# Seven half products for eight in part of a first FFN product, with sums and copies moved to GpSimd

## The chip, the cores and the metric

The kernel runs on one core of a Trainium2 chip. The metric is the device time of one execution in microseconds (us), as the median of several runs. The engines are TensorE (PE; PEld is its weight load), VectorE (DVE), ScalarE (ACT), GpSimd (POOL) and SyncE (SP). Each runs its own instructions in order and waits on semaphores for the others.

## The reference

Attention for 8 batches of 8 heads, with 512 local and 32 global tokens of head dimension 64. Local tokens see the global ones and a window of 32 on both sides; global tokens see everything. The result, 4352 tokens of 512 values, goes through a feed-forward network:

```
s_ll = where(|i - j| <= 32, scale * q_l @ k_l.T, -1e9);  s_lg = scale * q_l @ k_g.T
out_l = softmax([s_lg, s_ll]) @ [v_g, v_l]
out_g = softmax(scale * q_g @ [k_g, k_l].T) @ [v_g, v_l]
x = [out_g, out_l] as (tokens, 512)
h = x @ w_in                 # 512 -> 2048
g = h / (1 + exp(-1.702 h))
out = g @ w_out              # 2048 -> 512
```

The matrix products take bf16 operands and sum in f32. Inputs and outputs are f32.

## The kernel before

A batch has 512 local tokens; the global tokens of all batches are one more "batch" of 256, number B = 8, done last. Attention works on head groups of four heads; batch b has two, `a` and `c` (class `Wide`, lines 500 to 604). For each: `Tk` and `Tq` transpose loaded keys and queries on DVE, `kcopy`, `qcopy` and `ext` copy parts of them into place, `S` forms scores on PE in two rounds, `X` takes the exponential on ACT, `M` multiplies by the window mask (DVE, or POOL where `eng` says so), `U` and `Gm` multiply by the values on PE, `R` forms reciprocals of the sums (DVE), `XL` and `G` write the normalised result into `xL[b]`, the activations of the FFN, and `xG`.

The FFN has two stages per batch.

- The *h stage* (lines 1087 to 1109): sixteen blocks, `h_step(i, fc)`, of four matmuls of 128 x 128 weights by 512 tokens (`h_mm`, L615), then gelu on ACT into `gTs[i][:, fc]` (`gelu`, L620). Between blocks stand transposes and copies for the second head group of batch i+1 and the first of batch i+2, and sums of gelu outputs, `g_sums`.
- The *output stage*, `phase_o(i)` (lines 1017 to 1085): the second product, as two `Pair`s. A `Pair` forms a 2 x 2 block product with seven half products instead of eight (Strassen's scheme in Winograd-like form); it needs sums of blocks of w_out (`wsum`, formed once) and of gelu outputs. `g_sums(i, lo, hi, which)` forms four kinds of the latter for groups lo to hi-1, where group g holds blocks 2g and 2g+1: kinds 0, 1 and 3 are 256 columns per group, kind 2 is 512 (L696, L699, into `gs0` to `gs3`). Products 3 and 4 need no sum, product 1 kind 0, product 6 kind 1, products 5 and 2 kind 2, and product 7 kind 3. Products 3 and 4 are added up by `m3` (a copy on ACT) and `z` (DVE) before products 5 and 2 may go on into the same PSUM bank (`px`); `zm` reads product 1 before 6 and 7 may add to `py`; `sub`, `evict` and `add` finish. Between the products stand the attention steps of batch i+1 and the first scores of batch i+2.

The order of work is written out by hand: with `manual_schedule` each engine's queue holds its instructions in the order in which the program calls them. So an instruction that waits holds all behind it on its engine. PSUM is given out in turn: four banks of `psP` (tag `p`: `hp`, `ov`, `og`, `px`, `py`) and two double banks (`spair`, scores). `gT` and the four `gs` tiles exist once, `ob` (the output rows) three times.

POOL's queue in the middle of the kernel holds the mask multiply of the first head group's first round (`a2.M(0, nc.gpsimd)`, L1053) and the DMA issues of `loads_after` (L961): nine for the values of batch i+3, and for batch i+4 the two of keys and queries, which wait until the h stage's transposes have freed their buffer.

The steps that the change touches, as they stand in an h stage of batches 2 to 7 and in `phase_o`:

```
if fc == 1: c.Tk(); c.Tq(); c.ext((3,))
if fc in (3, 5, 7): c.ext(((3, 5, 7).index(fc),), on_act)
if fc == 9: a2.T(); transpose_g(2 * i + 4, 2 * i + 6); a2.ext()
if fc in (4, 8, 12): g_sums(i, fc // 2 - 2, fc // 2)
if fc == 13: g_sums(i, 6, 7)
...
a.UG(); c.S(0); a.R(); g_sums(i, 7, 8, (0,)); a.XL(0); g_sums(i, 7, 8, (1, 2))
a.XL(1); g_sums(i, 7, 8, (3,)); p0.mm(3, 4, 1); c.X(0); p0.m3(); p0.z(); a.G()
c.M(0); c.S(1); c.X(1); p0.mm(6); p0.zm(); c.M(1); p0.mm(5, 2); p0.sub(); p0.evict(); p0.mm(7)
```

Of the kernel before, what the change touches and what calls it, by code (L numbers as in the profile page):

```python
# [12 lines left out]
F32 = mybir.dt.float32  # L13
# [7 lines left out]
def kernel(  # L21
# [12 lines left out]
    nc = tc.nc  # L34
# [77 lines left out]
    def on_act(out_, in_):  # L112
        nc.scalar.activation(out_, in_, AF.Copy)  # L113
# [170 lines left out]
    def spair():  # L284
        return [psS.tile([128, 2, 512], F32, name="s4", tag="s%d" % i) for i in range(2)]
# [4 lines left out]
    class Quad:  # L290
        def __init__(self, Q):
            self.Q = Q
            self.b, self.u = divmod(Q, 2)
            if self.u == 0:
                xL[self.b] = att.tile([128, NKC, Sl], BF16, name="xL", bufs=2)
            self.x = xL[self.b]
            self.v = v_view(self.b, 5 if self.b else 4)[:, self.u]
            self.qt = qtiles[Q % 4]
            self.q = self.qt.bitcast(BF16).rearrange("p t (r e) -> p t r e", e=2)
            self.qg = qgT[:, Q, :32].bitcast(BF16).rearrange("p (s e) -> p s e", e=2)  # L300
            self.kg = kgT[:, Q].bitcast(BF16).rearrange("p (s e) -> p s e", e=2)
            self.E = [None, None]
            self.bk = {}
            self.st = {}
            self.pt = None
            self.gr = 1
# [312 lines left out]
    def gelu(out_, in_):  # L619
        nc.scalar.activation(out_, in_, AF.Gelu_apprx_sigmoid)  # L620
# [12 lines left out]
    def exp_table():  # L633
        nc.scalar.activation(spot[:, 0:1], spot[:, 1:2], AF.Exp)
# [5 lines left out]
    def h_step(i, fc):  # L640
# [4 lines left out]
        h_mm(i, fc, hp, range(NKC))  # L645
        h_act(i, fc, hp)

    def o_mm(i, st, out=True, part=range(4)):
        tci, f4 = divmod(st, 4)
        first = (i, tci) not in ops  # L650
        if first:
            ops[i, tci] = pbank("op")
        op = ops[i, tci]
        for fc in [4 * f4 + n for n in part]:
            nc.tensor.matmul(op, lhsT=gTs[i][:, fc, tci * 128 : tci * 128 + 128],  # L655
                             rhs=w_out_sb[:, fc, :], start=(first and fc == 4 * f4), stop=(fc == FC - 1))
        if f4 == 3 and 3 in part and out:
            o_out(i, tci, op)
# [18 lines left out]
        t = gTs[i].rearrange("p (g e) t -> p g e t", e=2)  # L677
        return [t[:, :, e, h * n // 2 : h * n // 2 + n // 2] for h in range(2) for e in range(2)]

    def g_sums(i, lo, hi, which=(0, 1, 2, 3)):  # L680
        n = width(i)
        if i not in sums:
            if i < B:
                sums[i] = [moe.tile([128, FC // 2, w * HT], BF16, name="gs%d" % k)
                           for k, w in enumerate((1, 1, 2, 1))]
            else:
                room = [ld.tile([128, 2, 16 * D], BF16, name=x).rearrange("p a b -> p (a b)")
                        for x in ("rk", "rq", "rk")]
                sums[i] = [x.rearrange("p (g t) -> p g t", g=FC // 2)
                           for x in (room[0][:, :1024], room[0][:, 1024:], room[1], room[2][:, :1024])]  # L690
        a11, a12, a21, a22 = parts_of(i)
        t = gTs[i].rearrange("p (g e) t -> p g e t", e=2)
        g = slice(lo, hi)
        for k in which:
            if k == 2:
                nc.vector.tensor_tensor(sums[i][2][:, g, :n], t[:, g, 0, :n], t[:, g, 1, :n], ALU.add)  # L696
            else:
                x, y, op = {0: (a11, a22, ALU.add), 1: (a21, a11, ALU.subtract), 3: (a12, a22, ALU.subtract)}[k]
                nc.vector.tensor_tensor(sums[i][k][:, g, : n // 2], x[:, g], y[:, g], op)  # L699

    class Pair:
        def __init__(self, i, tt, banks=None):
# [4 lines left out]
        def mm(self, *ks):  # L707
            i, tt = self.i, self.tt
            n = width(i) // 2
            a11, a12, a21, a22 = parts_of(i)  # L710
            s = sums[i]
            for k in ks:
                lv, rv, where = {
                    1: (s[0], wsum[0], 2), 2: (s[2][:, :, n : 2 * n], b11, 1), 3: (a11, wsum[1], 0),
                    4: (a22, wsum[2], 1), 5: (s[2], b22, 0), 6: (s[1], wsum[3], 3), 7: (s[3], wsum[4], 2),
                }[k]
                if self.apart:
                    out_ = self.banks[where][:, :HM]
                else:
                    if k == 3:  # L720
                        self.x = self.banks[0] if self.banks else pbank("px")
                    if k == 1:
                        self.y = self.banks[1] if self.banks else pbank("py")
                    out_ = (self.y if where > 1 else self.x)[:, where % 2 * HM : where % 2 * HM + HM]
                for g in range(FC // 2):
                    nc.tensor.matmul(out_, lhsT=lv[:, g, tt * 128 : tt * 128 + 128], rhs=rv[:, g, :],  # L726
                                     start=(g == 0 and k in ((1, 3, 4, 6) if self.apart else (1, 3))), stop=(g == FC // 2 - 1 and k in (2, 5, 6, 7)),
                                     skip_group_check=True)

        def m3(self, eng="act"):  # L730
            self.zz = moe.tile([128, 2, HM], F32, name="zz")
            if eng == "act":
                on_act(self.zz[:, 0], self.x[:, :HM])
            else:
                nc.vector.tensor_copy(self.zz[:, 0], self.x[:, :HM])

        def z(self):
            nc.vector.tensor_add(self.zz[:, 0], self.zz[:, 0], self.x[:, HM:])

        def zm(self):  # L740
            nc.vector.tensor_add(self.zz[:, 1], self.zz[:, 0], self.y[:, :HM])
# [5 lines left out]
        def sub(self):  # L747
            nc.vector.tensor_sub(self.zz, self.zz, self.x.rearrange("p (h m) -> p h m", h=2))  # L748

        def add(self):  # L750
            nc.vector.tensor_add(self.ob[:, 0:4:3], self.zz, self.y.rearrange("p (h m) -> p h m", h=2))
# [265 lines left out]
    def phase_o(i):  # L1017
        b = i + 1
        a, c = nq[b]
        a2, c2 = quads_of(b + 1)  # L1020
        p0, p1 = Pair(i, 0), Pair(i, 1)
        exp_table()
        a.UG()
        c.S(0)
        a.R()
        g_sums(i, 7, 8, (0,))
        a.XL(0)
        g_sums(i, 7, 8, (1, 2))
        a.XL(1)
        g_sums(i, 7, 8, (3,))  # L1030
        p0.mm(3, 4, 1)
        c.X(0)
        p0.m3()
        p0.z()
        a.G()
        c.M(0)
        c.S(1)
        c.X(1)
        p0.mm(6)
        p0.zm()  # L1040
        c.M(1)
        p0.mm(5, 2)
        p0.sub()
        p0.evict()
        p0.mm(7)
        p0.add()
        p0.store()
        if a2:
            c.UG()
            c.R()  # L1050
            a2.S(0)
            a2.X(0)
            a2.M(0, nc.gpsimd)  # L1053
            loads_after(i + 1)
        else:
            pt = spair()
            c.U(0, bank(pt, 0))
            c.U(1, bank(pt, 2))
            c.U(2, bank(pt, 3))
            c.Gm(bank(pt, 1))  # L1060
            c.R()
        c.XL(0)
        if a2:
            c.XL(1)
            c.G()
        p1.mm(3, 4)
        p1.m3()
        p1.z()
        if not a2:
            c.XL(1)  # L1070
            c.G()
        p1.mm(1, 6)
        p1.zm()
        if a2:
            a2.S(1)
            a2.X(1)
        p1.mm(5, 2)
        p1.sub()
        p1.evict()
        gelu_table()  # L1080
        p1.mm(7)
        p1.add()
        if a2:
            a2.M(1)
        p1.store()

    for i in range(1, B):
        if i > 1:
            for fc in range(FC):
                h_step(i, fc)  # L1090
                if i == 2 and fc == 0:
                    weight_sums(1, 2)
                if i + 1 < B:
                    c = nq[i + 1][1]
                    if fc == 1:
                        c.Tk()
                        c.Tq()
                        c.ext((3,))
                    if fc in (3, 5, 7):
                        c.ext(((3, 5, 7).index(fc),), on_act)  # L1100
                    if fc == 9 and i + 2 < B:
                        a2 = quads_of(i + 2)[0]
                        a2.T()
                        transpose_g(2 * i + 4, 2 * i + 6)
                        a2.ext()
                if fc in (4, 8, 12):
                    g_sums(i, fc // 2 - 2, fc // 2)
                if fc == 13:
                    g_sums(i, 6, 7)
        if i == 1:  # L1110
            phase_o1()
        elif i + 1 < B:
            phase_o(i)
# [88 lines left out]
```

## Time and profile before

| what | us |
|---|---|
| median of 3 runs | 287.18 (286.78 to 289.01) |
| the profiled execution | 288.3 |
| its span, first to last instruction | 286.5 |
| PE busy | 278.6 |
| DVE busy | 204.7 |
| ACT busy | 183.9 |
| POOL busy | 95.1 |
| one h stage of batches 3 to 7, PE | 13.8 |
| one output stage of batches 2 to 5, PE | 17.7 |
| granted TensorE clock, mean | 0.998 of full speed |

The span is the profiled execution's own; what lies around it is 1.8 us. Lines such as L615 are lines of the kernel as printed above; a helper's line stands for all its calls. In a line of a timeline the first number is the start in us from the span's start, the second the time until the last of the merged instructions ends; in brackets stands how long the engine had been idle and what released it. In the chain of waits each line is a piece of the path that ended last: start, length, engine, what is written, source line and the number of instructions.

### The profile page before, as it was taken

The page shows a single profiled execution, that of the slowest core. Times are in us where ns is not written, and L with a number is a line of the kernel's source. Part 1 is how long each engine was busy: PE and PEld are TensorE (multiplying, and loading weights), DVE is VectorE, ACT ScalarE, POOL GpSimd, SP SyncE. Part 2 cuts the span into 40 slices and gives each one's busy share as a digit, 9 for nine tenths or more (in the row PEclk, how much of TensorE's full clock was granted, in tenths as well). Part 3 has the DMA queues.
Part 4 walks back from the last instruction along what each step waited for, and adds up shares of the span by engine and source line. Part 5 has one row for each costly group of instructions (what it writes and reads, how often), then busy time and mean ns, then how long its engine had stood idle before and what let it go on. Part 6 is the DMA issues. An engine that isn't in the chain of part 4 may idle for free.

```text
span 286.5 us, 8846 instructions
## 1 busy us (share of the span) xinstructions
PE 278.6 (97%) x3727; PEld 179.0 (62%) x3727; DVE 204.7 (71%) x494; ACT 183.9 (64%) x297; POOL 95.1 (33%) x142
## 2 busy tenths in 40 slices
PE   7899999989999999999999999999999999999995
PEld 6554445434554478646884488647874589448884
DVE  6680468678689899579957998679957697363352
ACT  3857657558678775688458783878468761864331
POOL 8974550765936100940068002910040000000001
PEclk9999999999999999999999999999999999999999
DMA  7999995899999901794029903880122002200213
GB/s 203 174 194 210 203 141 83 148 212 134 152 168 194 152 3 39 82 188 83 2 77 153 159 6 76 79 87 5 28 51 73 2 3 76 73 0 2 73 35 115
DMA packets 59351, 28.23 MB, mean 99 GB/s; under 512 B 47472, under 2 KB 49776, under 8 KB 59312
## 3 DMA queue, kind: packets, MB, share of 16 engines
q0 software_dynamic: 51760, 17.83, 55.1%
q1 hardware_dynamic: 7120, 9.18, 11.6%
q10 hardware_dynamic: 432, 0.66, 0.7%
q8 instruction: 29, 0.48, 0.7%
q14 instruction: 10, 0.08, 0.1%
HBM read 36.31 MB, written 8.91 MB: 158 GB/s over the span
## 4 chain that ended last, share of the span: by engine, by line
PE 77%; DMA 10%; POOL 7%; issue 3%; DVE 1%; ACT 1%; POOLq 0%
PE hp L615 33%; PE px L726 13%; PE py L726 9%; PE x L726 6%; PE op L655 5%; PE s L560 5%; PE ov L586 5%; DMA rq<-in_q_l_dram 4%; DMA w_out_sb<-in_moe_w_out_dram 3%; DMA rk<-in_k_l_dram 2%; POOL w_in_sb L260 2%; POOL v L250 1%; POOL mask L225 1%; POOL v L98 1%; PE og L597 1%
## 5 line engine op out<-in xcount | busy, mean ns | idle before, releaser
L615 PE MATMUL hp<-xL,w_in_sb 128*128 128x512 bf16 x480 | 105.6, 379 | 1.5 <-ACT gT L620 1.3
L615 PEld LDWEIGHTS <-w_in_sb 128*128 128x128 bf16 x576 | 56.0, 98 | 61.6 <-issue 2.0
L620 ACT ACTIVATE gT<-hp 128x512 bf16<-128x512 f32 x120 | 69.7, 597 | 23.6 <-PE hp L615 22.0
L571 ACT ACTIVATE e<-s 128x1016 bf16<-128x1016 f32 (+1 forms) x56 | 53.2, 1003 | 25.3 <-PE s L560 25.3
L726 PEld LDWEIGHTS <-gs 128*128 128x128 bf16 x480 | 46.3, 98 | 6.4
L699 DVE TENSOR_TENSOR gs<-gT 128x512 bf16<-128x512 bf16 (+1 forms) x90 | 30.3, 363 | 17.5 <-ACT gT L620 17.3
L576 POOL TENSOR_TENSOR e<-e,mask 128x1760 bf16<-128x1760 bf16 x4 | 13.3, 3319 | 83.4 <-ACT e L571 83.4
L98 POOL DMA_DIRECT2D v<-in_v_l_dram x40 | 31.1, 780 | 14.9 <-PE og L597 4.3
L726 PE MATMUL py<-wsum,gs 128*128 128x256 bf16 x240 | 30.3, 273 | 0.0
L655 PE MATMUL op<-w_out_sb,gT 128*128 128x512 bf16 x128 | 29.5, 380 | 0.0
L576 DVE TENSOR_TENSOR e<-e,mask 128x1712 bf16<-128x1712 bf16 (+1 forms) x24 | 25.2, 1048 | 4.2 <-ACT e L571 4.1
L512 DVE STREAM_TRANSPOSE kT<-rk 128x512 f32<-128x512 f32 x14 | 14.6, 1045 | 17.4 <-DMA rk<-in_k_l_dram 17.4
L759 POOL DMA_DIRECT2D out_dram<-ob x2 | 1.2, 597 | 68.2 <-ACT ob L113 68.0
L655 PEld LDWEIGHTS <-gT 128*128 128x128 bf16 x128 | 11.8, 98 | 14.0
L726 PEld LDWEIGHTS <-gT 128*128 128x128 bf16 x192 | 18.0, 98 | 2.9
L726 PE MATMUL px<-w_out_sb,gT 128*128 128x256 bf16 x160 | 19.2, 273 | 0.0
L726 PE MATMUL px<-w_out_sb,gs 128*128 128x256 bf16 x160 | 19.1, 273 | 0.0
L471 DVE TENSOR_TENSOR xL<-ov,rs 128x512 bf16<-128x512 f32 x27 | 17.9, 686 | 0.7 <-PE ov L438 0.3
L696 DVE TENSOR_TENSOR gs<-gT 128x1024 bf16<-128x1024 bf16 (+1 forms) x30 | 17.3, 578 | 0.0
L560 PEld LDWEIGHTS <-kT 32*128 32x128 bf16 x672 | 12.5, 93 | 6.8 <-issue 5.7
L113 ACT ACTIVATE ob<-px 128x512 f32<-128x512 f32 x10 | 6.0, 598 | 15.2 <-DVE zz L748 15.2
L560 PE MATMUL s<-q,kT 32*128 32x160 bf16 (+1 forms) x448 | 14.7, 246 | 0.0
(154 smaller groups left out, 359.7 us busy)
## 6 DMA issues: line engine op xcount, KB each, us to landing
out_dram<-ob SPq DMA_DIRECT2D x128, 64.0 KB, 2.4
rq<-in_q_l_dram POOLq DMA_DIRECT2D x5, 512.0 KB, 8.0
rk<-in_k_l_dram POOLq DMA_DIRECT2D x5, 512.0 KB, 10.4
v<-in_v_l_dram POOLq DMA_DIRECT2D x24, 96.0 KB, 4.8
w_in_sb<-in_moe_w_in_dram POOLq DMA_DIRECT2D x8, 256.0 KB, 8.1
w_out_sb<-in_moe_w_out_dram POOLq DMA_DIRECT2D x4, 512.0 KB, 10.4
rk<-in_k_l_dram POOLq DMA_DIRECT2D x5, 256.0 KB, 7.9
rq<-in_q_l_dram POOLq DMA_DIRECT2D x5, 256.0 KB, 8.0
```

The lines of the kernel that those rows point to most:

```text
L98: nc.gpsimd.dma_start(out=vt[0:n, hs, c, :D], in_=vs[FIRST[c] : FIRST[c] + n, hs])
L471: nc.vector.tensor_mul(self.x[:, 2 * self.u + h, :], self.st[1 + h], self.st["rs"])
L512: nc.vector.transpose(flat[:, 0:Sl].rearrange("p (r t) -> p t r", t=16), loaded[self.b][0][:, self.u].bitcast(F32))
L560: nc.tensor.matmul(bank(self.ps, j)[:, at : at + n], lhsT=self.k[p, KEYS[c] : KEYS[c] + 128, e], rhs=qs[p, :, :, e], start=(e == 0), stop= ...
L571: nc.scalar.activation(self.E[rnd][:, 2 * i : 2 * i + 2, :n], self.ps[i][:, :, :n], AF.Exp, scale=scale)
L576: eng.tensor_mul(e, e, mask[:, rnd : rnd + 1, :n].to_broadcast([128, 4, n]))
L615: nc.tensor.matmul(hp[:, : width(i)], lhsT=w_in_c[:, fc // 4, kc, fc % 4 // 2, :, fc % 2], rhs=(xL[i] if i < B else xG)[:, kc, :], start=( ...
L620: nc.scalar.activation(out_, in_, AF.Gelu_apprx_sigmoid)
L655: nc.tensor.matmul(op, lhsT=gTs[i][:, fc, tci * 128 : tci * 128 + 128], rhs=w_out_sb[:, fc, :], start=(first and fc == 4 * f4), stop=(fc = ...
L696: nc.vector.tensor_tensor(sums[i][2][:, g, :n], t[:, g, 0, :n], t[:, g, 1, :n], ALU.add)
L699: nc.vector.tensor_tensor(sums[i][k][:, g, : n // 2], x[:, g], y[:, g], op)
L726: nc.tensor.matmul(out_, lhsT=lv[:, g, tt * 128 : tt * 128 + 128], rhs=rv[:, g, :], start=(g == 0 and k in ((1, 3, 4, 6) if self.apart els ...
```

## The change

For batches 3 to 7, blocks 4 to 7 of the h stage (groups 2 and 3) are formed with seven half products per pair of blocks (class `HPair`) and not as four `h_step`s: 28 matmuls of 256 columns for 16 of 512. This takes sums of blocks of w_in (`h_weight_sums`, once, on POOL, in the output stage of batch 2's program; they lie in `early`, a buffer that is only used at the start and in the last batch), sums of blocks of `xL` (`x_sums`, four instructions on DVE, called in `phase_o` after `p1.zm()`), and four further DVE instructions and a copy on ACT per batch (`z`, `zm`, `sub`, `add`, `m3`). Gelu of these four blocks is two instructions of 1024 columns, `inner` from PSUM and `outer` from the `ob` buffer that held the sums.

The h stage of batches 3 to 7 is written anew (`h_some`). Kinds 2 and 3 of the sums of groups 0 and 1, kinds 1, 2 and 3 of groups 2 to 5 and kind 2 of group 6 go to POOL; groups 2 to 5 are summed in one instruction per kind after `outer`. The copies `kcopy`, `qcopy` and part 3 of `ext` for the second head group of batch i+1, and all copies for the first of batch i+2, go from DVE to POOL, the latter after the sums. The h stage of batch 2, the sums of group 7 and the last batch are as they were.

```diff
+    HG = (2, 3)
+    w_h = w_in_sb.rearrange("p o k (g m e) -> p o k g m e", m=128, e=2)[:, 1]
+    w11, w12, w21, w22 = (w_h[:, 2 * k : 2 * k + 2, :, :, e] for e in range(2) for k in range(2))
...
+    def h_weight_sums(eng=nc.gpsimd):
+        for t, x, y, op in zip(wh, (w11, w21, w11, w21, w12), (w22, w22, w12, w11, w22),
+                               (ALU.add, ALU.add, ALU.add, ALU.subtract, ALU.subtract)):
+            eng.tensor_tensor(t, x, y, op)
...
+    def x_sums(i):
...
+        for o, x, y, op in zip(xs["d"], (x11, x12, x21), (x22, x22, x11), (ALU.add, ALU.subtract, ALU.subtract)):
+            nc.vector.tensor_tensor(o, x, y, op)
+        nc.vector.tensor_tensor(xs["s"], t[:, :, :HT], t[:, :, HT:], ALU.add)
+        xs["r"] = (x11, x22)
+
+    class HPair:
+        def __init__(self, i):
+            self.i = i
+            self.x, self.y = spair()
+            self.zz = moe.tile([128, 4, HM], F32, name="ob", bufs=3).rearrange("p (u h) t -> p u h t", u=2)
+
+        def mm(self, *ks):
+            for k in ks:
+                lv, rv, where = {
+                    1: (wh[0], xs["d"][0], 2), 2: (wh[1], xs["r"][0], 1), 3: (w11, xs["d"][1], 0),
+                    4: (w22, xs["d"][2], 1), 5: (wh[2], xs["r"][1], 0),
+                    6: (wh[3], xs["s"][:, 0:2], 3), 7: (wh[4], xs["s"][:, 2:4], 2),
+                }[k]
+                for u in range(2):
+                    t = self.y if where > 1 else self.x
+                    for kc in range(2):
+                        nc.tensor.matmul(t[:, u, where % 2 * HT : where % 2 * HT + HT],
+                                         lhsT=lv[:, kc, u], rhs=rv[:, kc, :],
...
+        def m3(self):
+            on_act(self.zz[:, :, 0], self.x[:, :, :HT])
+
+        def z(self):
+            nc.vector.tensor_add(self.zz[:, :, 0], self.zz[:, :, 0], self.x[:, :, HT:])
+
+        def zm(self):
+            nc.vector.tensor_add(self.zz[:, :, 1], self.zz[:, :, 0], self.y[:, :, :HT])
+
+        def sub(self):
+            nc.vector.tensor_sub(self.zz, self.zz, self.x.rearrange("p u (h t) -> p u h t", h=2))
+
+        def add(self):
+            nc.vector.tensor_add(self.zz, self.zz, self.y.rearrange("p u (h t) -> p u h t", h=2))
...
+        def inner(self):
+            gelu(self.out()[:, :, 1:3], self.x.rearrange("p u (h t) -> p u h t", h=2))
+
+        def outer(self):
+            gelu(self.out()[:, :, 0:4:3], self.zz)
...
-    def g_sums(i, lo, hi, which=(0, 1, 2, 3)):
+    def g_sums(i, lo, hi, which=(0, 1, 2, 3), eng=nc.vector):
...
-                nc.vector.tensor_tensor(sums[i][2][:, g, :n], t[:, g, 0, :n], t[:, g, 1, :n], ALU.add)
+                eng.tensor_tensor(sums[i][2][:, g, :n], t[:, g, 0, :n], t[:, g, 1, :n], ALU.add)
...
-                nc.vector.tensor_tensor(sums[i][k][:, g, : n // 2], x[:, g], y[:, g], op)
+                eng.tensor_tensor(sums[i][k][:, g, : n // 2], x[:, g], y[:, g], op)
...
         exp_table()
+        if i == 2:
+            h_weight_sums()
         a.UG()
...
         p1.zm()
+        x_sums(i + 1)
         if a2:
             a2.S(1)
...
+    def h_some(i):
+        c = nq[i + 1][1] if i + 1 < B else None
+        a2 = quads_of(i + 2)[0] if i + 2 < B else None
+        pool = nc.gpsimd
+        for fc in range(4):
+            h_step(i, fc)
+            if c and fc == 1:
+                c.Tk(False)
+                c.Tq(False)
+                c.kcopy(pool.tensor_copy)
+                c.qcopy(pool.tensor_copy)
+                c.ext((3,), pool.tensor_copy)
+            if c and fc == 3:
+                c.ext((0,), on_act)
+        g_sums(i, 0, 2, (0,))
+        p = HPair(i)
+        p.mm(3, 4)
+        p.m3()
+        p.z()
+        p.mm(1, 6)
+        p.zm()
+        if a2:
+            a2.Tk(False)
+        g_sums(i, 0, 2, (1,))
+        h_step(i, 8)
+        p.mm(5, 2)
+        p.inner()
+        p.sub()
+        p.mm(7)
+        p.add()
+        g_sums(i, 0, 2, (2, 3), pool)
+        h_step(i, 9)
+        if c:
+            c.ext((1,), on_act)
+        h_step(i, 10)
+        if c:
+            c.ext((2,), on_act)
+        h_step(i, 11)
+        p.outer()
+        if a2:
+            a2.Tq(False)
+            transpose_g(2 * i + 4, 2 * i + 6)
+        g_sums(i, 2, 6, (0,))
+        g_sums(i, 2, 6, (1,), pool)
+        h_step(i, 12)
+        h_step(i, 13)
+        g_sums(i, 6, 7, (0, 1, 3))
+        for k in (2, 3):
+            g_sums(i, 2, 6, (k,), pool)
+            if k == 2:
+                g_sums(i, 6, 7, (2,), pool)
+        if a2:
+            a2.kcopy(pool.tensor_copy)
+            a2.qcopy(pool.tensor_copy)
+            a2.ext(copy=pool.tensor_copy)
+        h_step(i, 14)
+        h_step(i, 15)
```

## The prediction

> **What bounds the kernel now.** I read the page first. TensorE (PE) is busy for 97% of the span, and nothing else comes near:
>
> ```profile
> span 286.5 us, 8846 instructions
> PE 278.6 (97%) x3727; PEld 179.0 (62%) x3727; DVE 204.7 (71%) x494; ACT 183.9 (64%) x297; POOL 95.1 (33%) x142
> ```
>
> Next the chain of waits in order of time, for batch 3 (its h stage from 119, its output stage from 133):
>
> ```profile
> 119.07 13.81 PE hp L615 x64
> 132.88 1.21 PE ov L586 x57
> 134.09 0.16 PE og L597 x20
> 134.25 0.57 PE s L560 x24
> 134.82 1.85 PE px L726 x16
> 136.67 0.87 PE py L726 x8
> 137.55 0.56 PE s L560 x22
> 138.11 0.98 PE py L726 x8
> 139.09 1.75 PE px L726 x16
> 140.83 0.87 PE py L726 x8
> ```
>
> The reader is to see that piece follows piece without a gap: PE is the path, and a wait put in front of any of these lengthens the kernel in full. An h stage is 64 matmuls in 13.81, so 216 ns for one of 512 columns; eight of 256 columns take 0.87, so 109 ns. The lines also fix when each product asks for its sums, counted from the end T of the h stage: product 1 at 3.79, 6 at 5.23, 5 and 2 at 6.21, 7 at 7.95, the second head group's attention product at 8.83, the next batch's scores at 10.2.
>
> Last, the timelines of DVE and of POOL (GpSimd), since the change sets these two side by side. POOL's only compute in the middle is the mask multiply, and DVE has just two instructions beside it, each with one input in PSUM:
>
> ```profile
> 114.29 3.32 POOL L576 TENSOR_TENSOR e<-e,mask 128x1760 bf16<-128x1760 bf16 x1 [20.41 <-ACT e L571]
> ...
> 115.82 0.42 DVE L741 TENSOR_TENSOR zz<-zz,py 128x256 f32<-128x256 f32 x1 [0.77 <-PE py L726]
> 118.23 0.69 DVE L748 TENSOR_TENSOR zz<-zz,px 128x512 f32<-128x512 f32 x1 [2.00 <-PE px L726]
> ```
>
> And one DVE copy, beside a POOL instruction that issues a DMA, and without one a few batches later:
>
> ```profile
> 122.51 0.81 POOL L98 DMA_DIRECT2D v<-in_v_l_dram  x1
> ...
> 122.87 0.48 DVE L545 COPY kT<-kgT 128x256 bf16<-128x256 bf16 x1
> ...
> 217.34 0.22 DVE L545 COPY kT<-kgT 128x256 bf16<-128x256 bf16 x1
> ```
>
> The copy needs 0.22, but beside POOL it ends at 123.35, just after POOL's instruction (123.32). The same happens at 154.43 (ends 154.91, POOL 154.88) and 185.93 (186.41, POOL 186.38). So a DVE instruction can be held until the end of a POOL instruction.
>
> **The change part by part.** Times within a stage count from its first matmul; before, the stage of batch 3 begins at 118.9.
>
> *PE work.* Sixteen 512-column matmuls (16 x 216 = 3.45 us) become 28 of 256 columns (28 x 109 = 3.05 us). The twelve more weight loads (98 ns each) stay beside the matmuls, as in the output products, which run at 109. That is 0.41 per batch, **2.0 us in five batches**, and all there is to gain.
>
> *ACT.* Four gelus of 512 columns (597 ns) become two of 1024 (1018 ns in the row from `s`), plus a copy (598): +0.2 per batch beside 13 us of PE work in which ACT is busy 11. No cost, as long as its inputs are on time.
>
> *DVE.* New: z and zm (0.69 each), sub and add over 1024 f32 columns (the rows 256 at 410 and 512 at 688 ns give 1.09 ns a column, so 1.24 each), and x_sums (three of 0.42 and one of 0.68, 1.7 in overlap). Gone: nine copies (2.0) and the sums that go to POOL (4.6). About even in busy time; placement decides.
>
> *POOL.* The multiply row gives 3317/1760 = 1.885 ns a column. Sums of groups 0 and 1: 1536 columns, 2.9. Then, after the outer gelu, in this order: A (kind 1, groups 2 to 5) 1.93, B (kind 2) 3.86, C (kind 2, group 6) 0.97, D (kind 3) 1.93, together 8.7. Copies, by the mask-copy rows (192 columns 534 ns, 128 columns 418 ns): 1.81 ns a column and 0.19 each, so 2.1 for the second head group and 3.3 for the next batch's first, with the DMA issues of the loads ahead of the former (POOL is on them until 6.4 into the h stage). With the multiply (3.3) and the issues (7.7) this is 29 us of POOL in a period of 31.5 (13.8 and 17.7).
>
> *If POOL and DVE run side by side.* Gelu 3 ends at 4.25, the copy at 5.2, z at 5.9; products 5 and 2 ask at 6.06: no wait. The outer gelu ends at 11.65. A to D end at 13.6, 17.5, 18.5, 20.4; T is 13.4. Product 5 wants C's result at 19.6 and product 7 D's at 21.35: hidden with 1 us to spare. The copies end at 23.65 and the scores want them at 23.6: 0.2 in each of three batches. x_sums fit in the 2.0 us in which DVE waits for px. Sum: -2.0 + 0.6 = -1.4.
>
> *If a two-input DVE sum is held like that copy.* No row has a DVE instruction with both inputs in SBUF beside a reading POOL instruction, so I bound it. Low end: no hold; DVE's sums beside POOL's DMA issues keep their length (two in 0.76, at 154.69 as at 217.69). High end: hold to POOL's end, as the copies. I take the second: issuing a DMA only writes a few descriptors, whereas A to D stream SBUF for their whole length, and even the issue held a DVE instruction. One batch, then:
> - x_sums wait for the multiply's end, 1.3 before the stage, and end at +0.35, so sub, ACT's copy and the gelus are 1.0 late: gelu 3 ends at 5.2, the part-3 copy at 6.1, z at 6.85. Products 5 and 2 wait **0.8**. T becomes 14.2.
> - Outer gelu to 12.4, DVE's sum of kind 0 to 13.0, A to 14.9; the three sums of group 6 wait for A and end at 15.5; B runs 15.5 to 19.4. Group 7's kind 0 stands behind R (free at 17.2) and gets through at 19.6; product 1 wanted it at 18.0: **1.7**.
> - C holds the next two sums until 20.6, D holds kind 3 until 23.1, so z of the first output pair, queued behind, ends at 23.6; products 5 and 2 wanted it at 22.1: **1.6**.
> - Two mask multiplies meet POOL's copies (half a copy, 0.5, each): zm at 26.2 for product 7 at 25.45, **0.8**, and **0.5** before the second head group's attention product.
>
> That is 5.4 per batch for batches 3 to 6. In batch 7 product 5 of the tail wants C (20.5) at 19.1: 1.4. The weight sums (five of 512 columns, 4.8 on POOL, from 93.9 when batch 5's load is issued) meet batch 2's sums, after which DVE is full until 102.2; 2 us of holds against 1.1 of slack at product 1: 1.0. Sum: 4 x 5.4 + 1.4 + 1.0 - 2.0 = **+22.0**.
>
> Ends for this case. Lowest: DVE is first each time except at B (1.7 + 0.8 per batch): 10 + 1 - 2 = +9. Highest: the two engines strictly alternate, so group 6's three sums interleave with B, C and D: s0 at 22.7 rather than 19.6, and per batch 0.8 + 4.7 + 1.1 + 1.1 + 0.4, with 1.0 for a late gelu at the stage's end, 9.1; 36.4 + 4 + 2 - 2 = +40.
>
> The Trainium skill, page "SBUF — State Buffer", section "Who interferes with whom", speaks against this change: a VectorE instruction with two SBUF inputs and a GpSimd instruction that reads SBUF exclude each other, and the later one stands until the earlier has ended. By that rule the sum is +22.0, the second walk; by the DMA row it is -1.4, the first. The trace agrees with its hold-to-the-end (0.48 for 0.22, three times) and with two-input sums being free beside DMA issues; the pair that matters no run here shows yet.
>
> **Where the sum stands.** The profiled execution took 288.3 (span 286.5 and 1.8 around it); the median is 287.18, 1.1 less. +22.0 gives 310.3 on the profiled execution and **309.2** as median.
>
> **The rivals.**
> 1. *Held (the forecast), 0.66*: 309.2, from 296 (+9) to 327 (+40). For it: the copies. Against it: DVE sums beside DMA issues run free, so not everything is held.
> 2. *Side by side, 0.25*: 285.8, from 285.2 (no wait at the scores) to 289. The other side: PE keeps its chain, sums on POOL stay hidden. It decides if DVE's sums keep 0.28 to 0.68 beside POOL; it needs holds under about 1 us per batch, the slack of product 1.
> 3. *Side by side, but POOL is the bound, 0.07*: its sums take longer than the multiply's row. From 9.65 instead of 8.7 on (2.1 ns a column), product 7 waits for D; at half again the row (13.0) it is 3.4 a batch, 15 to 17 in five: 303. Against it: the four multiplies agree within 10 ns (3315 to 3324).
> 4. *Faster by more than 1%, 0.02*: needs 2.9, and the PE work gives 2.0.
>
> **How the numbers follow.** 1% is about what a measurement of this kernel can tell from no change. Rivals 1 and 3 are slower by more than that, 0.73 with a little from 2 above 290 making 0.74; same 0.24; faster 0.02. The likeliest case alone: 296 to 327. The 8-in-10 range reaches over the side-by-side case: 285.4 to 322, which leaves out the top of case 1 and the bottom of case 2.
>
> **What would show it.** Right: DVE's bf16 sums with durations of 1 to 4 us, each ending with a POOL instruction's end; gaps on PE before `px` and `py` with DVE sums as releaser; h stages at 14.2 and output stages near 22 instead of 17.7. Wrong: those sums at 0.28 to 0.68 while POOL adds, and the h stages at 13.4 with output stages at 17.7 (side by side), or waits of PE on POOL's sums directly (POOL bound). The 0.41 is wrong if the 28 half products take other than 3.05.

## The result and the profile after

| | before | after |
|---|---|---|
| median, us | 287.1 (286.54 to 289.01, 6 runs) | 335.7 (334.12 to 336.57, 6 runs) |
| profiled execution, us | 288.3 | 335.15 |
| its span, us | 286.5 | 333.2 |
| granted TensorE clock, mean | 0.998 | 0.944 |

The ratio is 1.1678, with a 95% interval of 1.1645 to 1.171: 48.6 us slower. The forecast had the sign and the mechanism, and less than half of the size; 335.7 lies above its range.

The page of after, first its sums and the row of the clock:

```profile
span 333.2 us, 9013 instructions
PE 292.2 (88%) x3787; PEld 192.1 (58%) x3787; DVE 260.4 (78%) x454; ACT 182.9 (55%) x292; POOL 178.5 (54%) x207
...
PEclk9999999999997899978999789996999969998999
```

PE falls from 97% to 88%. It has less work and yet 13.6 us more busy time, and the row of the clock has a dip once per batch. DVE has fewer instructions and 56 us more busy time. Where that lies is told by the costliest groups, shapes kept apart, first of before and then of after (count | busy us, mean ns of one):

```profile
L699 DVE TENSOR_TENSOR gs<-gT 128x256 bf16<-128x256 bf16 x36 | 9.5, 279 | 0.8 <-ACT gT L620 0.7
```

```profile
L770 DVE TENSOR_TENSOR gs<-gT 128x256 bf16<-128x256 bf16 x36 | 44.0, 1250 | 1.4 <-ACT gT L620 1.4
```

The same 36 sums on DVE take 1250 ns instead of 279, which is 34.5 of the 56 us. POOL's sums take somewhat more than its multiply's row had given (2048 columns 4.09 in the mean, forecast 3.86; 512 columns 1.20, forecast 0.97). What PE waits for, in after (us in total, times, longest):

```profile
PE px L797 <- DVE sT L462: 27.5, 5, 5.8
PE x L797 <- DVE gs L770: 4.7, 1, 4.7
PE ov L586 <- ACT gT L620: 2.3, 2, 1.2
```

In before the same view lists no wait of PE from 87 to 257 us. Batch 4 shows how the first of these comes about. The timeline of DVE in after, at the end of its h stage:

```profile
181.22 1.86 DVE L770 TENSOR_TENSOR gs<-gT 128x256 bf16<-128x256 bf16 x1 [0.28 <-ACT gT L620]
183.01 4.13 DVE L770 TENSOR_TENSOR gs<-gT 128x256 bf16<-128x256 bf16 x1
187.06 1.23 DVE L770 TENSOR_TENSOR gs<-gT 128x256 bf16<-128x256 bf16 x1
188.22 0.70 DVE L462 STREAM_TRANSPOSE sT<-ov 128x512 f32<-128x512 f32 x1
```

The timeline of POOL in after, same place (the sums A, B and C of the prediction):

```profile
180.29 2.64 POOL L770 TENSOR_TENSOR gs<-gT 128x1024 bf16<-128x1024 bf16 x1 [3.92 <-ACT gT L620]
182.89 4.10 POOL L767 TENSOR_TENSOR gs<-gT 128x2048 bf16<-128x2048 bf16 x1
186.95 1.20 POOL L767 TENSOR_TENSOR gs<-gT 128x512 bf16<-128x512 bf16 x1
```

And the timeline of PE in after:

```profile
180.75 0.55 PE L586 MATMUL ov<-e,ones 128*32 128x128 bf16 x24 [1.16 <-ACT gT L620]
...
188.97 3.57 PE L797 MATMUL px<-w_out_sb,gT 128*128 128x256 bf16 x16 [5.84 <-DVE sT L462]
192.34 1.61 PE L797 MATMUL py<-wsum,gs 128*128 128x256 bf16 x8
```

Each of group 6's three DVE sums ends 0.15 us after one of POOL's (183.08 and 182.93, 187.14 and 186.99, 188.29 and 188.15), so the three take 7.07 instead of 0.84. Behind them in DVE's queue stands `R`, whose first transpose (L462) reads the bank of `ov`. Product 3 writes into that same bank, since four banks are given out in turn, and waits 5.84. Then comes something else: 16 `px` matmuls take 3.57, not the 1.92 of before in the same view, with no wait between them. Two stretches of after, batch 4, as busy time by engine (PE, PEld, DVE, ACT, POOL), then the granted clock:

```profile
182.90:188.97 6.07, 0.23 (x16) 0.15 (x5) 6.04 (x5) 2.58 (x4) 6.07 (x4) 0.81 0.00 0
188.97:190.50 1.53, 1.52 (x8) 1.06 (x8) 1.50 (x4) 0.00 (x0) 1.53 (x2) 0.50 0.00 0
```

After the wait the clock is at half.

Where the 46.7 us between the two spans lie, by the first matmul of each h stage:

| stretch | before | after | difference |
|---|---|---|---|
| start to the h stage of batch 2 | 87.41 | 85.35 | -2.1 |
| batch 2 | 31.50 | 39.03 | +7.5 |
| batch 3 | 31.49 | 41.29 | +9.8 |
| batch 4 | 31.50 | 41.14 | +9.6 |
| batch 5 | 31.50 | 40.38 | +8.9 |
| batch 6 | 30.23 | 37.17 | +6.9 |
| h stage of batch 7 | 13.81 | 13.42 | -0.4 |
| tail | 29.06 | 35.42 | +6.4 |

The first row is not the change's: no instruction differs up to there, and in r4 below, whose instructions are the same so far, it is 90.2. So runs are compared by these periods, from one h stage to the next. Batch 4's 9.6 is 5.84 before product 3, 2.2 of slow clock (16 matmuls +1.65, the next 8 +0.57), 1.16 before `UG`, 0.19 before products 5 and 2, 0.6 in pieces under 0.35, less the 0.41.

### The profile page after: what moved, and what is told of

It reads as the page before. It is cut to its first block, busy times and chain, and to the rows that moved or that the text cites. A ratio compares the mean times of both kernels' runs of the same rounds, so it can differ in the third digit from the quotient of the medians.

```text
span 333.2 us, 9013 instructions
## 1 busy us (share of the span) xinstructions
PE 292.2 (88%) x3787; PEld 192.1 (58%) x3787; DVE 260.4 (78%) x454; ACT 182.9 (55%) x292; POOL 178.5 (54%) x207
## 5 line engine op out<-in xcount | busy, mean ns | idle before, releaser
L615 PE MATMUL hp<-xL,w_in_sb 128*128 128x512 bf16 x400 | 89.8, 379 | 0.2 <-DVE xL L471 0.2
L615 PEld LDWEIGHTS <-w_in_sb 128*128 128x128 bf16 x496 | 48.5, 98 | 48.9 <-issue 0.4
L770 DVE TENSOR_TENSOR gs<-gT 128x256 bf16<-128x256 bf16 (+2 forms) x60 | 62.7, 1068 | 11.3 <-ACT gT L620 11.3
L620 ACT ACTIVATE gT<-hp 128x512 bf16<-128x512 f32 x100 | 55.8, 597 | 16.5 <-PE hp L615 15.5
L797 PE MATMUL px<-w_out_sb,gT 128*128 128x256 bf16 x160 | 27.5, 344 | 27.5 <-DVE sT L462 27.5
L767 POOL TENSOR_TENSOR gs<-gT 128x1024 bf16<-128x1024 bf16 (+2 forms) x15 | 37.4, 2504 | 19.8 <-ACT gT L620 19.8
L797 PEld LDWEIGHTS <-gT 128*128 128x128 bf16 x192 | 21.8, 116 | 34.1 <-issue 27.4
L770 POOL TENSOR_TENSOR gs<-gT 128x1024 bf16<-128x1024 bf16 (+1 forms) x15 | 30.2, 2010 | 18.8 <-ACT gT L620 18.8
L797 PE MATMUL py<-wsum,gs 128*128 128x256 bf16 x240 | 33.7, 291 | 0.0
L113 ACT ACTIVATE zz<-px 128x256 f32<-128x256 f32 x10 | 3.9, 386 | 37.1 <-PE px L797 37.1
L726 PEld LDWEIGHTS <-gT 128*128 128x128 bf16 x128 | 11.8, 98 | 13.9
```

Source lines behind the costliest of these rows:

```text
L615: nc.tensor.matmul(hp[:, : width(i)], lhsT=w_in_c[:, fc // 4, kc, fc % 4 // 2, :, fc % 2], rhs=(xL[i] if i < B else xG)[:, kc, :], start=( ...
L767: eng.tensor_tensor(sums[i][2][:, g, :n], t[:, g, 0, :n], t[:, g, 1, :n], ALU.add)
L770: eng.tensor_tensor(sums[i][k][:, g, : n // 2], x[:, g], y[:, g], op)
```

## The experiments

Theories. *Hold*: DVE's two-input sums are held by POOL's sums, and PE waits for what is queued behind them. *POOL late*: PE waits for POOL's results themselves. *DVE full*: DVE has too much to do, hold or none. *Clock*: the long wait lowers the clock, which costs a second time. For the order in which the two engines pass, *gap*: a held sum moves on only while the other engine is between columns or reads, so its time goes with its size; and *lock*: it stands until POOL's instruction ends, whatever its size. The label of each run is in its heading; edits are against after unless said. Of the runs, r9_sums_act and r9b_sums_pool_copies stand for four executions each, the others for one. The kernel before took 287.7 beside r1 to r8 and 287.3 beside the others.

| run | us | period of batch 3 | waits before `px`, longest |
|---|---|---|---|
| after | 335.7 | 41.3 | 5.8 |
| r1_weight_sums_dve | 331.9 | 39.6 | 5.8 |
| r2_sums_dve | 306.7 | 33.9 | 2.3 |
| r3_plain_blocks | 323.0 | 40.7 | 6.7 |
| r4_write_only | 300.6 | 32.0 | none |
| r5_fill | 326.2 | 39.4 | 0.4 |
| r6_group6_behind_R | 338.8 | 42.1 | none (6.4 before `py`) |
| r7_before_pool_sum | 303.5 | 36.5 | 3.5 |
| r8_before_pool_memset | 294.9 | 34.2 | 2.5 |
| r10_wide_sum | 334.4 | 41.0 | 6.0 |
| r11_half_sums | 344.0 | 43.6 | 8.5 |
| r9_sums_act | 292.1 | 33.1 | none |
| r9b_sums_pool_copies | 294.1 | 33.1 | none |

For r2, r4 and r6 the last column leaves out batch 2, where the weight sums on POOL make `px` wait 4.9.

**Sums of gelu outputs back on DVE (r2_sums_dve).**

```diff
-        g_sums(i, 0, 2, (2, 3), pool)
+        g_sums(i, 0, 2, (2, 3))
...
-        g_sums(i, 2, 6, (1,), pool)
+        g_sums(i, 2, 6, (1,))
```

and so for the other two calls.

> The changed kernel with all sums of gelu outputs on DVE, in the same places; copies and weight sums stay on POOL. Theory H: DVE's sums of 256 columns are back at 0.28 (1.25 on average in the changed kernel), the 5.8 us waits for px in batches 3 to 6 go with the slow matmuls behind them; what is left is the weight sums' 6.6 and up to 1 us per batch for DVE's fuller queue: 292 to 300. Theory D: DVE has 4.6 us more to do in each of five batches, so not faster than 335.7, rather 350. Theory P would also fall to below 300, so this run does not tell H from P.

306.7, 29 us less than after, although batch 2 starts 3.1 later: most of the loss is these sums. DVE's sums of 256 columns are back at 307 ns. But it missed 292 to 300: DVE is busy 31.1 of 33.9 per batch (some 1.7 of it held by POOL's multiply and copies) and PE still waits 2.3 before product 3. So *DVE full* is not the cause in after, but a second limit right behind it.

**POOL writes but does not read (r4_write_only).** In place of each sum, POOL copies two elements, so that the order stays, and then fills the result twice with zeros.

```diff
+            if eng is nc.gpsimd:
+                for gg in {min(lo + 1, hi - 1), hi - 1}:
+                    nc.gpsimd.tensor_copy(spot_p, t[0:1, gg, 1, n - 2 : n])
+                for _ in range(2):
+                    nc.gpsimd.memset(sums[i][k][:, g, : n if k == 2 else n // 2], 0.0)
+                continue
```

> The changed kernel with each POOL sum of gelu outputs replaced by tiny POOL copies that wait for the gelu outputs as the sum does, and two POOL memsets of the sum's output, which only write; kinds 2 and 3 of most groups, and kind 1 of groups 2 to 5, are therefore zero and not sums. POOL is busy about as long (a memset of 880 columns took 0.82, so two of n columns 1.86 ns a column; the sums took 2.0 to 2.4). Theory H in the form that it is POOL's reading that holds DVE: DVE's sums are back at 0.28 to 0.69 and the px waits go, 292 to 297 with the weight sums still on POOL. Theory H in the form that any busy POOL holds DVE: no change, 330 to 336. Theory P (late results): POOL is as late as before, no change, 330 to 336. The Trainium skill, page SBUF - State Buffer, section Who interferes with whom, says that a two-input VectorE instruction contends with a GpSimd instruction that reads SBUF and not with one that only writes it; that is the first form.

300.6. The result is zero where the sums belong, so this kernel tells about time alone. The timelines of DVE and of POOL in this kernel, in the same stretch:

```profile
177.89 0.28 DVE L776 TENSOR_TENSOR gs<-gT 128x256 bf16<-128x256 bf16 x1
178.09 0.42 DVE L773 TENSOR_TENSOR gs<-gT 128x512 bf16<-128x512 bf16 x1
```

```profile
178.20 1.80 POOL L770 MEMSET gs<- 128x2048 bf16 x1
```

The memset shown is the second of two that follow each other from 176.35 on. Sums of 0.28 and 0.42 pass while POOL writes without a break; the period is 32.0, and PE's waits for POOL's results sum to 1.8 in four batches, at most 0.5. *POOL late* falls, and it is POOL's reading that holds a two-input DVE sum. The Trainium skill, page "SBUF — State Buffer", section "Who interferes with whom", says this: a VectorE instruction with two SBUF inputs contends with a GpSimd instruction that reads SBUF, not with one that only writes. The trace agrees, with 1250 ns beside reading and 280 beside writing.

**Without the half products (r3_plain_blocks).** The sixteen blocks are `h_step`s again, with no `x_sums` and no weight sums; the sums on POOL stay.

```diff
-        p = HPair(i)
-        p.mm(3, 4)
...
+        h_step(i, 4)
+        h_step(i, 5)
```

> The changed kernel without the seven half products: blocks 4 to 7 are four plain blocks again, no sums of xL and of w_in are formed, but sums and copies stay on POOL as in the changed kernel. Theory H: the three sums of group 6 still stand behind POOL's A, B and C and R behind them, so some 9 us per batch in batches 3 to 6 stay and about 5 in batch 7; the weight sums' 6.6 go and the 2.0 of PE work comes back: 328 to 332. Theory D: DVE is rid of 5.5 us per batch, so near 290. Theory P: as H, since POOL's work stays.

323.0, 5 below the range expected; the period is 40.7 against 41.3, so the half products are not what costs. Here a hold is longest. DVE's and POOL's timelines in this kernel:

```profile
128.17 9.34 DVE L770 TENSOR_TENSOR gs<-gT 128x1024 bf16<-128x1024 bf16 x1 [4.34 <-ACT gT L620]
```

```profile
127.64 2.11 POOL L770 TENSOR_TENSOR gs<-gT 128x1024 bf16<-128x1024 bf16 x1
129.72 5.16 POOL L767 TENSOR_TENSOR gs<-gT 128x2048 bf16<-128x2048 bf16 x2
134.85 2.11 POOL L770 TENSOR_TENSOR gs<-gT 128x1024 bf16<-128x1024 bf16 x1
```

A sum of 0.69 stands through four POOL sums and ends at 137.51, half a microsecond after the last: POOL went on to its next instruction three times without letting it in. In batches 5 to 7 the same sum beside the same four of POOL takes 1.85 and gets in after the first.

**The weight sums on DVE (r1_weight_sums_dve).**

```diff
-        if i == 2:
-            h_weight_sums()
         a.UG()
...
         p0.store()
+        if i == 2:
+            h_weight_sums(nc.vector)
```

> The changed kernel, but the five sums of blocks of w_in are formed on DVE, behind the store of the first output pair of batch 2, and not on POOL. Theory H (a DVE sum with two SBUF inputs stands while POOL reads, and PE waits behind it): in batch 2 one DVE sum lasted 6.96 us instead of 0.69, PE then waited 4.91 for px and ran 16 matmuls in 3.57 instead of 1.85; all of that goes, so 6.5 less than the changed kernel's 335.7, about 329. Theory P (PE waits for results that POOL delivers late) and theory D (DVE has simply too much to do): no POOL result is late in batch 2 and DVE gets 1.7 us more work, so no gain, 335 to 338.

331.9, less than hoped for, though batch 2 also starts 2.2 later: its period goes from 39.0 to 35.9. The wait of 4.91 before its first product 3 is gone and the 16 matmuls run in 1.92, which is the hold. But I had put 3.09 us of DVE work ahead of the second head group's `R`, and its product 3 now waits 2.50 and meets the slow clock. Three stretches from the end of that wait on, in this kernel:

```profile
114.84:116.30 1.46, 1.46 (x9) 1.13 (x9) 1.32 (x3) 0.00 (x0) 1.46 (x1) 0.65 0.54 139
116.30:117.80 1.50, 1.50 (x9) 1.06 (x7) 1.43 (x5) 0.00 (x0) 1.50 (x2) 0.50 0.16 40
117.80:119.00 1.20, 1.20 (x9) 0.91 (x7) 0.59 (x2) 0.38 (x1) 1.20 (x2) 0.63 0.00 0
```

If the clock is either 1.00 or 0.50, it was at half for 1.02 + 1.50 + 0.89 = 3.4 us, beginning after the wait had ended.

**PE kept busy through the wait (r5_fill).** 96 matmuls of 128 columns whose result is not used, ahead of product 3.

```diff
+        fill(96, a.st["og"][:, 128:256], True)
         p0.mm(3, 4, 1)
```

> The changed kernel with 96 extra matmuls of 128 columns on PE in each of phase_o(2) to phase_o(6), between the first scores of the second head group and product 3; they write unused columns of the bank of og and nothing reads them. In the changed kernel PE waits there 5.84 us and then runs 16 matmuls in 3.57 and 8 in 1.6 to 1.8, at a granted clock of 0.50, in place of 1.85 and 0.87. Theory C (the idle time itself lowers the granted clock, and that is a second cost of the wait): the wait shrinks by about the 5 us that the extra matmuls take, the 24 matmuls behind it are back at 2.8, so 2.4 less in each of five batches, 323 to 325. Rival (the slow matmuls come from what DVE and POOL do at that time): no change, 335 to 337.

326.2. The timeline of PE in this kernel, batch 4:

```profile
179.20 5.53 PE L183 MATMUL og<-warm 128*128 128x128 bf16 x96
185.12 1.91 PE L797 MATMUL px<-w_out_sb,gT 128*128 128x256 bf16 x16 [0.39 <-DVE sT L462]
```

With the same hold but no idle PE, the 16 matmuls take 1.91: *clock* holds. The period falls by 1.9, to 39.4.

**Group 6's sums behind `R` (r6_group6_behind_R).**

```diff
         a.R()
+        if i > 2:
+            g_sums(i, 6, 7, (0, 1, 3))
...
-        g_sums(i, 6, 7, (0, 1, 3))
```

> The changed kernel with DVE's three sums of group 6 moved behind R (in the last batch directly ahead of the sums of group 7). Theory H: R no longer stands behind held sums, so the wait of product 3 for px goes (5.84 in batches 3 to 6), but the same sums and those of group 7 are held behind R in turn until POOL is through with B, C and D (about 8 us after the stage's end), so product 1, 6 or 5 waits instead: the period of batches 3 and 4, 41.3 in the changed kernel, becomes 38 to 41. Rival (only the bank of px matters, and DVE catches up): 31.5 to 34.

338.8: it missed, and is no better than after. The timeline of PE in this kernel:

```profile
143.55 1.92 PE L797 MATMUL px<-w_out_sb,gT 128*128 128x256 bf16 x16
151.85 1.86 PE L797 MATMUL py<-wsum,gs 128*128 128x256 bf16 x8 [6.38 <-DVE xL L471]
```

`R` is now in time and product 3 doesn't wait; product 1 does, behind the same held sums, for `xL` and with the slow clock. The wait moves with the sums.

**The kernel before with one POOL sum (r7_before_pool_sum, edit against before).** Nothing reads its result.

```diff
+    def pool_extra(i):
...
+        nc.gpsimd.tensor_tensor(o, t[:, 2:6, 0, :], t[:, 2:6, 1, :], ALU.add)
...
+                    if 2 < i < 7:
+                        pool_extra(i)
```

> The kernel before the change with one more POOL instruction in each of batches 3 to 6: the sum of blocks 4 to 11 (2048 columns, as B) into an unused buffer, called behind the sums of group 6; nothing waits for its result. Theory H: it lasts 3.9 to 4.1 us from block 11's gelu on, DVE's sums of groups 4, 5 and 6 stand for up to that long, R and with it px come 2 to 3 us late, and the granted clock may fall behind the wait: 2 to 5 us in each of four batches, 295 to 307. Rival (the cost in the changed kernel comes from the half products or from late results on POOL): no change, 287 to 288.5, and DVE's sums at 0.28 to 0.68.

303.5: the periods of batches 3 to 6 are longer by 5.0, 5.2, 3.6 and 2.6, for a sum that no engine waits for. What is held was not what I expected. DVE's and POOL's timelines in this kernel:

```profile
128.71 4.09 DVE L507 COPY qc<-q 128x384 bf16<-128x384 bf16 x1
```

```profile
128.61 4.06 POOL L678 TENSOR_TENSOR early<-gT 128x2048 bf16<-128x2048 bf16 x1 [4.83 <-ACT gT L620]
```

It is a copy, of 0.26 in before, and the transposes, sums and `R` stand behind it. In batch 6, which has no such copies, it is a two-input sum of 512 columns (4.29 for 0.42).

**The same with writes alone (r8_before_pool_memset, edit against r7_before_pool_sum).**

```diff
-        nc.gpsimd.tensor_tensor(o, t[:, 2:6, 0, :], t[:, 2:6, 1, :], ALU.add)
+        nc.gpsimd.tensor_copy(spot_p, t[0:1, 5, 1, 510:512])
+        for _ in range(2):
+            nc.gpsimd.memset(o, 0.0)
```

> As the run with one more POOL sum in the kernel before, but with a tiny POOL copy that waits for block 11's gelu and two POOL memsets of the same 2048 columns (3.6 us together), which only write. If it is POOL's reading that holds DVE: no change, 287 to 288.5, DVE's sums at 0.28 to 0.68. If any busy POOL holds DVE: as with the sum, 295 to 307.

294.9, at the lower edge of what any busy POOL was to give, and not the 287 to 288.5 of reading alone. Writes do hold DVE's copies. The timeline of DVE in this kernel, beside two memsets from 129.15 to 132.81:

```profile
129.08 1.99 DVE L507 COPY qc<-q 128x384 bf16<-128x384 bf16 x1
```

The next three copies stand until the second memset has ended (1.43 to 1.59 for 0.17 to 0.20). Batch 6, with no such copies, has DVE's sums at 0.28 to 0.68 beside the memsets and a period of 30.22, that of before (30.23); with POOL's sum in r7 it was 32.82. So there are two kinds: a two-input sum is held by reading, a copy by reading or writing. The section "Who interferes with whom" of the Trainium skill's page "SBUF — State Buffer" has VectorE's copies, in their faster modes, contend with GpSimd for the whole instruction; the trace agrees, 1.99 for 0.26. r4 is free of this: there these copies are on POOL itself.

**One sum of two groups, and sums of half the size (r10_wide_sum, r11_half_sums).**

```diff
-        g_sums(i, 6, 7, (0, 1, 3))
+        g_sums(i, 5, 7, (0,))
+        g_sums(i, 6, 7, (1, 3))
```

> The changed kernel, but DVE's first sum of group 6 (kind 0, 256 columns) also forms group 5 again and so has 512 columns. In the changed kernel the three sums of 256 columns end one after each of POOL's A, B and C, while one of 1024 columns in batch 2 stood through five POOL sums in a row (6.96 us). Theory G (a held DVE sum moves only in the short gap between two POOL instructions, and about 256 columns fit into a gap): the 512-column sum needs the gaps behind A and behind B and ends with B, 4 us later than now; the next two end behind C and D, R comes about 2 us later, the wait for px grows from 5.8 to about 8 and the total by 8 to 10, to about 345. Theory L (whoever waits gets the port when the other's instruction ends, whatever the length): no change, 334 to 337.

```diff
-        g_sums(i, 6, 7, (0, 1, 3))
+        for k in (0, 1, 3):
+            half_sums(i, k)
```

Here `half_sums` forms kind k of group 6 in two instructions of 128 columns.

> The changed kernel with each of the three sums of group 6 in two halves of 128 columns. Theory G: two halves fit into one gap, so six instructions end as three did: no change beyond 1 us, 334 to 338. Theory L: each instruction passes behind one POOL instruction, so the six need A, B, C, D and two of the copies behind them: R comes 2 to 3 us later in batches 3 to 6, 343 to 348.

The sum of 512 columns is held 1.99, as that of 256 was (1.86), and nothing else moves: 334.4. The six of 128 columns pass one behind each POOL instruction. DVE's timeline in r11_half_sums:

```profile
185.34 4.08 DVE L778 TENSOR_TENSOR gs<-gT 128x128 bf16<-128x128 bf16 x1
189.35 1.18 DVE L778 TENSOR_TENSOR gs<-gT 128x128 bf16<-128x128 bf16 x1
```

Product 3 waits 8.5 rather than 5.8. In this place *gap* falls and *lock* holds: what counts is how many instructions stand in the queue, not their columns. *Lock* is not the whole rule, though, since the sum of 9.34 in r3 let three ends of POOL instructions go by.

**The half products with POOL kept from reading beside DVE's sums (r9_sums_act, r9b_sums_pool_copies).** All these sums go back to DVE but for two kinds of groups 0 and 1, which POOL forms while DVE has transposes and PSUM operands; the weight sums are made at the start on DVE; `R` comes first. The copies for batch i+2 are on ACT in the output stage (r9_sums_act) or on POOL early in the h stage (r9b_sums_pool_copies, which also takes those two kinds from POOL). The core of it:

```diff
-        g_sums(i, 2, 6, (1,), pool)
...
-        for k in (2, 3):
-            g_sums(i, 2, 6, (k,), pool)
...
+        g_sums(i, 6, 7, (0,))
+        g_sums(i, 2, 7, (1,))
...
+            g_sums(i, 2, 8, (2,))
...
+            a2.kcopy(on_act)
+            a2.qcopy(on_act)
```

> A version that keeps the half products and avoids the hold: the sums of w_in on DVE in its idle time behind batch 0's blocks; all sums of gelu outputs on DVE except kinds 2 and 3 of groups 0 and 1, which POOL forms while DVE does transposes and operations on PSUM; R ahead of kinds 2 and 3 of the other groups; the copies for the next batch's first head group on ACT in the output stage. Theory H with DVE and ACT just full: periods of 31.1 to 32 against 31.49 of the kernel before, 285 to 290. If theory H leaves something out, px waits stay: above 292.

> As the run with the copies on ACT, but those copies on POOL, called behind the transposes so that they lie beside DVE's sub and add, and kinds 2 and 3 of groups 0 and 1 on DVE. Theory H: POOL's copies are through before DVE's sums start or hold them for less than 1 us; DVE has 0.9 us more per batch: periods of 31.3 to 32.5, 286 to 292.

292.14 (291.93 to 292.55), ratio 1.0173 (1.0148 to 1.0199), and 294.11, ratio 1.0232 (1.0175 to 1.029); both have periods of 33.1 in batches 3 to 5, and both missed their ranges by 2. The holds behind POOL's sums and the slow clock are gone and the change still costs 1.6 per batch. One batch of before and one of r9_sums_act, columns as above:

```profile
118.91:150.40 31.49, 31.49 (x458) 21.32 (x456) 25.97 (x63) 22.00 (x35) 10.93 (x13) 1.00 0.64 89
```

```profile
117.81:150.90 33.09, 31.54 (x466) 22.62 (x468) 29.46 (x52) 23.43 (x40) 15.50 (x18) 1.00 0.61 85
```

DVE is busy 3.5 us more per batch and is at 89%. Of these, 1.3 are a hold that is left, as it is in after: the first of `x_sums` stands until POOL's mask multiply ends (1.73 for 0.42). No run takes this last hold away, so what the half products cost without any stays open. PE's waits are now short and many: 0.62 on `zm` before product 6, 0.51 on ACT's eviction within the second `UG`. No version that I tried beats the kernel before.

## Why the forecast had the sign and not the size

| step | forecast, us | measured, us |
|---|---|---|
| PE work per batch | -0.41 | -0.41 |
| before products 5 and 2 in the h stage (`z`) | 0.8 | 0.19 |
| late outer gelu, before `UG` | 0 (1.0 in the high end) | 1.14 and 1.16 in batches 3 and 4 |
| held sums, in the output stage | 1.7 + 1.6 | 5.84 in batch 4 |
| `zm`, second head group | 0.8 + 0.5 | 0 |
| slow clock, per batch | not in the sum | 2.2 in batch 4 |
| weight sums, batch 2 | 1.0 | 7.5 |
| tail | 1.4 | 6.4 |

- *Held, and not side by side*: right (r2, r4, r7). `x_sums` stood until the multiply's end as walked (1.74 for 0.42); of the 0.8 that this was to cost, 0.19 came. The choice was made by the DVE copy that a DMA issue held. r8 shows that this was the wrong relative: a copy is held by POOL's writes, while a two-input sum is free beside them. The row pointed the right way for another reason, and that was luck. Nor are two-input sums always free beside DMA issues, as the prediction took them to be (two in 0.76): in r9 one of 512 columns that starts 0.04 after such an issue takes 0.69 for 0.42 and ends with it.
- *PE saves 0.41*: right. The h stage of batch 7, in which PE waits for nothing, went from 13.81 to 13.42.
- *"The three sums of group 6 wait for A and end at 15.5"*: this is the step that failed. It let three queued sums through in one gap. In fact one passes after each POOL instruction, and the third ends at 22.6 into the stage (188.29 less 165.67). The high end had such an alternation, from B on, so it was within what I had bounded; the choice between the ends was wrong, and r11 shows the rule.
- *Where PE asks first*: the walk had product 1 as the first to wait. It is product 3, which needs no sum: its bank is freed by `R`, and `R` is queued behind the held sums. r6 confirms it. PE stands there so long that the later waits (1.6, 0.8, 0.5) are covered.
- *"Weight sums 1.0"*: mis-sized. One DVE sum of 0.69 stood 6.96 through all five of POOL's (5.69 in sum), and 4.91 of that came to PE, with the slow clock behind it; r1 removes this wait.
- *The clock* was in no term. It gives 2.2 in batch 4, and r5's periods are shorter than after's by 1.5 to 2.2; with batch 2 (2.2) and the tail (0.31 of 5 us) some 11 of the 48.6, at r5's mean of 1.8 per batch. Without these 11 the result would lie within the high end of +40, which already had the strict alternation.
- *Tail 1.4*: the same two errors. PE waits 4.68 for kind 0 of group 7, queued behind group 6's sums, and then runs at 0.69 of the clock for 5 us.
- *POOL as the bound*: no. Its copies were cheaper than forecast (0.24 to 0.56 each in batch 4), and r4 shows at most 0.5 of waiting on its results. A to D took 9.98 in batch 4 instead of 8.7, more than the 9.65 from which product 7 was to wait, but PE came so late that it did not.
- *ACT at no cost*: nearly. It was late by its inputs in `outer` because a sum of 512 columns ahead of `sub` and `add` was held for 3.02.
- Slips in the working that change no conclusion: POOL's terms add up to 28.0 and not 29; copies that end at 23.65 are 0.05 late for 23.6 and not 0.2; of the two DVE lines shown beside the mask multiply, the second (118.23) starts after it has ended (117.61); and rival 2 ends at 289, yet a little of its chance is counted above 290.

What stays open: why a held sum gets in after one POOL instruction in one place, and only after two (3.02), four (9.34) or five (6.96) in others. It is not the size alone (r10: 512 columns in after one; r3: the same 1024 columns in after four and after one). Who came first is not settled either: the one of 6.96 started at 91.12, before POOL's first weight sum (91.84), but just after a DMA issue on POOL (91.10 to 91.81).

## What to carry to other kernels

Work moved to an engine that looks idle has to be priced by what its operands share with the engine that it relieves: here a GpSimd instruction that read SBUF stopped a VectorE sum with two SBUF inputs until it had ended, sometimes for several such instructions in a row, and with it all that was queued behind. Count held instructions, not columns, and look behind them for what frees a PSUM bank, since that is what TensorE meets first. A wait of several microseconds on TensorE can cost twice, once for itself and once for the clock after it (1.9 per batch in r5).

## What the hardware showed that I had not expected

- A wait of 5.84 left TensorE's clock at 0.50. By the stretches of after's batch 4 it was there from 2.3 us before the wait's end (0.81 over 6.07) to 4.5 after it (1.53 and 1.80 at 0.50, then 1.60 at 0.62), 6.9 in all; in r1 3.4. A wait of 2.50 in r1 led to it, and one of 3.51 in r7's batch 5 did not (16 matmuls in 1.91). So the length of the wait alone does not decide. The traces show more of how a wait counts. The changes of the clock lie whole multiples of 3.41 us apart, and a wait is shared out between the steps of that grid. r7's 3.51 fell into two steps, with 1.55 and 1.96 of idle PE, and the clock stayed at 1.00. r1's 2.50 fell into one, and the next step was slow. Three waits of 2.3 in r2 gave 1.40 and 0.91, 1.65 and 0.65, 1.90 and 0.39, and only the third was followed by a slow step. In after, r1 to r7, r10 and r11, from 20 us on, steps at full clock with 2.06 or more of idle PE were all followed by 0.50, and none with 1.81 or less was; from 1.86 to 1.97 both occur. The Trainium skill, page "TensorE: Matmul & The Clock Gate", Part 1, has a free-running window of about 3.4 us over which activity is judged, and half the clock after an idle one. The stretches of 3.4 and twice 3.4 agree with that; that a window need not be wholly idle is what r1 adds.
- DVE's copies between SBUF tiles are held even by a memset on POOL (1.99 for 0.26), and its two-input sums are not (0.28 in r4 and r8).
- Held work does not always get the next turn: one DVE sum stood 9.34 us through four POOL instructions in a row.
